# The second mixture's first product as 15 block products over two weight tiles, three depth blocks and three groups of 256 tokens

## The chip, the cores and the metric

The kernel runs on one core of a Trainium2 chip. The metric is the device time of one execution in microseconds (us). The engines' names in the rows are: PE is TensorE (matmuls; PEld are its weight loads), DVE is VectorE, ACT is ScalarE, POOL is GpSimd, SP is SyncE, which here only issues transfers.

## What is computed

Three stages follow each other. A recurrent attention over B=4 sequences of S=768 tokens (8 heads of 48) gives 3072 rows of 384. The first mixture multiplies two products of these rows elementwise and takes them through two more matrices. The second mixture, which the change is about, has E=8 experts of 1024 hidden units and a gate that is normalised over rows and columns in turn, eight times (the Sinkhorn iterations):

```python
a = x @ w1                     # first mixture, x is 3072 x 384, w1 and w2 384 x 1024
b = x @ w2
x = (a * b @ w3) @ w_out       # 3072 x 384
...
logits = x @ w_gate            # second mixture, E = 8
P = np.exp(logits - logits.max())
for _ in range(8):
    P /= P.sum(1, keepdims=True) + 1e-09
    P /= P.sum(0, keepdims=True) + 1e-09
    P *= N / E
for e in range(E):
    h = np.maximum(x @ w1[e], 0.0)         # 3072 x 384 @ 384 x 1024
    out += P[:, e:e + 1] * (h @ w2[e])     # 3072 x 1024 @ 1024 x 384
```

All is float32. Each product of two blocks is made of three matmuls, since each factor is kept as a high part (rounded by ScalarE) and a low part (what is left, by GpSimd or VectorE): high by high, high by low, low by high.

## The kernel before

**The second mixture** is a loop over N=96 phases (expert e, slab sb, half dp). A slab is 512 tokens, 256 of each of two sequences; there are six. A weight tile i holds the columns of w1[e] and the rows of w2[e] for 256 hidden units; an expert has four, and a half has two. In a phase TensorE makes the hidden units of one slab for two weight tiles (called z, in PSUM tiles `zp`, three banks of 128 partitions by 512) and multiplies those of the phase before by w2 (called y, tiles `yp`). The depth 384 is three blocks of 128. Over two of the depth blocks, the two row blocks that a weight tile has and the two token groups, z goes by the seven products of Strassen's scheme in Winograd's form (P1 to P7); the third depth block adds four plain products (R11 to R22). That is 11 block products for each of the two tiles, 66 matmuls of 256 columns in a phase. y has 16 units of three matmuls of 384 columns. `phase` writes the order of TensorE out by hand: after each product `slot()` lets one queued piece of other work (`ex`) and one step of the Sinkhorn iterations (`sk`, from the third phase on) be issued, and `y_units(k)` puts k units of y between the products, so that the evacuation of a PSUM bank passes behind them.

**Evacuation.** ScalarE copies the first product of a phase out (`t`, L802) and takes the relu with rounding (`hh`, L779); VectorE forms the sums of the scheme (`u`, `vv`, `cc`, L786), the low halves (`hl`, L783) and, every second phase, four accumulations of y times the gate (`acc`, L894).

**Preparation of factors.** Both sides of the scheme need sums of blocks. For a weight tile `sp_w1a` makes four sums of 128x128 on GpSimd (L574 to L577), and `sp_w1b`, issued some slots later, the high halves on ScalarE (L591) and the low halves on GpSimd (L592): nine forms. For a slab of x, `sp_x_a` makes four sums of 128x256 on GpSimd (L619 to L622) and `sp_x_b` the high (L632) and low halves (L633), nine forms too. These are made once for each slab, in the first expert's phases (the first slab's at the end of the first mixture), stored to DRAM (`xd`) and loaded again into `xc` for each later expert, into two tiles in turn, 2304 KB a load. w2 is split by ScalarE (L605) and VectorE (L606).

**The end of the first mixture.** The last block of 384 tokens goes through eight slices (s=99 to 106), in each of which TensorE makes `pa` and `pb`, ScalarE copies `asb` (L423) and rounds `gh` (L437), VectorE multiplies `gs` (L436) and GpSimd makes `gl` (L438). Four more slices (s=107 to 110) make 72 matmuls `po` from `gh` and `gl`; the last three of their first third and the other 48 need the last `gl`. Beside this the first weight tiles and the first slab are prepared, in the order in which the slices are written.

Each engine works off its own instructions in the order written; a wait in one holds all that stand behind it on that engine. `reuse_waits="tile"` lets a tile's next use wait only for the last use of that tile.

## Time and profile before

| | us |
|---|---|
| device time, median of 3 runs | 2074.86 (2073.59 to 2075.13) |
| the profiled execution | 2072.34 |
| its span in the trace | 2070.2 |
| second mixture on TensorE: first z to last y | 502.14 to 2066.67 |
| one phase in steady state | 16.22 |

The span is the time from the first to the last instruction of the trace; 2.14 us of the profiled execution lie outside it. All times in the rows count from the span's start.

### The profile page before, as it was taken

To read this page: it belongs to the slowest core of one execution; us is meant where nothing else is said; L and a number is where in the kernel's file an instruction comes from. 1 tells how busy PE (TensorE), PEld (TensorE's weight loads), DVE (VectorE), ACT (ScalarE), POOL (GpSimd) and SP (SyncE) were. 2 spreads that over 40 slices of the span, in tenths; PEclk is the share of its full clock that TensorE was granted. 3 is DMA by queue.
4 is the path that set the end of the run, shared out by engine and by line. 5 is a ranking of instruction groups with operands and counts; after the bars stand their busy time and mean duration, and the time that the engine had idled before them with its cause. 6 is when DMAs were issued, how large, how long until landed. Compare 5 with 4: busy or idle time off the path is not lost.

```text
span 2070.2 us, 37109 instructions
## 1 busy us (share of the span) xinstructions
PE 2004.5 (97%) x16075; PEld 1954.4 (94%) x16075; DVE 1145.3 (55%) x1782; ACT 531.1 (26%) x916; POOL 487.4 (24%) x487
## 2 busy tenths in 40 slices
...
GB/s 251 182 141 94 89 91 100 102 40 92 107 92 92 108 92 47 91 152 47 92 63 137 91 47 128 73 91 92 108 92 47 92 152 47 92 63 122 106 78 31
DMA packets 45827, 199.55 MB, mean 96 GB/s; under 512 B 6176, under 2 KB 16480, under 8 KB 38496
## 3 DMA queue, kind: packets, MB, share of 16 engines
...
## 4 chain that ended last, share of the span: by engine, by line
PE 92%; DVE 5%; POOL 1%; issue 1%; ACT 1%; DMA 1%; SPq 0%; DVEq 0%; ACTq 0%; POOLq 0%
...
## 5 line engine op out<-in xcount | busy, mean ns | idle before, releaser
L84 PE MATMUL zp<-xc,w1h 128*128 128x256 f32 x4224 | 781.9, 280 | 0.9 <-ACT t L802 0.9
L84 PEld LDWEIGHTS zp<-xc,w1h 128*128 128x128 f32 x4224 | 691.3, 188 | 2.0 <-ACT t L802 1.4
L84 PE MATMUL zp<-xc,w1l 128*128 128x256 f32 x2112 | 594.2, 281 | 0.0
L84 PE MATMUL yp<-w2h,hh 128*128 128x384 f32 x1536 | 517.8, 337 | 0.0
L84 PE MATMUL yp<-w2l,hh 128*128 128x384 f32 x1536 | 516.6, 336 | 0.6 <-DVE w2l L606 0.6
L84 PE MATMUL yp<-w2h,hl 128*128 128x384 f32 x1536 | 516.2, 336 | 0.0
L84 PEld LDWEIGHTS zp<-xc,w1l 128*128 128x128 f32 x2112 | 398.1, 189 | 0.0
L779 ACT ACTIVATE hh<-cc 128x512 fp32r<-128x512 f32 x288 | 182.2, 633 | 797.6 <-DVE cc L786 797.6
L592 POOL TENSOR_TENSOR w1l<-w1raw,w1h 128x768 fp32r<-128x768 f32 x32 | 59.2, 1851 | 1087.8 <-ACT w1h L591 1087.8
L84 PEld LDWEIGHTS yp<-w2h,hh 128*128 128x128 f32 x1536 | 289.7, 189 | 0.4 <-issue 0.2
L84 PEld LDWEIGHTS yp<-w2l,hh 128*128 128x128 f32 x1536 | 288.8, 188 | 0.9 <-DVE w2l L606 0.9
L84 PEld LDWEIGHTS yp<-w2h,hl 128*128 128x128 f32 x1536 | 288.3, 188 | 0.0
L786 DVE TENSOR_TENSOR cc<-u,zp 128x512 f32<-128x512 f32 x192 | 131.9, 687 | 269.1 <-PE zp L84 269.1
L786 DVE TENSOR_TENSOR u<-t,zp 128x512 f32<-128x512 f32 x192 | 132.0, 688 | 200.0 <-PE zp L84 164.6
L783 DVE SCALAR_TENSOR_TENSOR hl<-cc,hh 128x512 fp32r<-128x512 f32 x288 | 198.7, 690 | 7.2 <-ACT hh L779 7.1
L894 DVE SCALAR_TENSOR_TENSOR acc<-yp,Pm,acc 128x384 f32<-128x384 f32 x168 | 103.4, 616 | 116.8 <-PE yp L84 116.8
L779 ACT ACTIVATE hh<-zp 128x512 fp32r<-128x512 f32 x96 | 57.5, 599 | 257.1 <-PE zp L84 257.1
L783 DVE SCALAR_TENSOR_TENSOR hl<-zp,hh 128x512 fp32r<-128x512 f32 x96 | 65.9, 686 | 74.5 <-ACT hh L779 74.3
L438 POOL TENSOR_TENSOR gl<-gs,gh 128x384 fp32r<-128x384 f32 x64 | 84.4, 1318 | 96.3 <-ACT gh L437 96.2
L84 PE MATMUL pa<-xhl,w1h 128*128 128x384 f32 x384 | 105.3, 355 | 1.4 <-DVE xhl L405 0.8
L84 PE MATMUL pb<-xhl,w2h 128*128 128x384 f32 x384 | 98.7, 338 | 1.9 <-ACT w2h L198 1.9
L786 DVE TENSOR_TENSOR vv<-u,zp 128x512 f32<-128x512 f32 x96 | 66.0, 688 | 49.8 <-PE zp L84 49.7
...
## 6 DMA issues: line engine op xcount, KB each, us to landing
xc<-xd SPq DMA_DIRECT2D x42, 2304.0 KB, 8.8
xd<-xc SPq DMA_DIRECT2D x6, 2304.0 KB, 6.9
...
```

What stands on the lines that cost most here:

```text
L84: nc.tensor.matmul(o, lhsT, rhs, start=start, stop=stop, **kw)
L438: nc.gpsimd.tensor_tensor(gl[:, f, :], gs, gh[:, f, :].bitcast(F32), op=ALU.subtract)
L592: nc.gpsimd.tensor_tensor(lo[:, d0:d0 + n, :], src, hi[:, d0:d0 + n, :].bitcast(F32), op=ALU.subtract)
L779: nc.scalar.activation(hh, src, AF.Relu)
L783: nc.vector.scalar_tensor_tensor(hl, src, 0.0, hh.bitcast(F32), op0=ALU.max, op1=ALU.subtract)
L786: nc.vector.tensor_tensor(o, a, b_, op=ALU.add)
L894: nc.vector.scalar_tensor_tensor(dst, ya[t], Pm[:, tt, e:e + 1], dst, op0=ALU.mult, op1=ALU.add)
```

## The change

z is made by a scheme of 15 block products over a matrix of 2 by 3 blocks (two row blocks of a weight tile, three depth blocks) and one of 3 by 3 (three depth blocks, three groups of 256 tokens), where plain multiplication needs 18. A slab is now one whole sequence, 768 tokens; there are 16 pairs of weight tiles (k) by four slabs (sb), so N=64 phases. A phase has 15 products of 6 matmuls (128x256) and 24 units of y of 3 matmuls (128x384). `ORDER` is the order of the products, `WA` and `XC` say which blocks make the two factors of each. The products fall into four groups by that order (four, four, four, three); the factor forms of a group lie in one tile (`w1c{k}{g}`, `xc{g}`).

What moves with it:

- `combine` and `split` now stand together: a call of `sp_w1(i, g)` or `sp_x(sb, g)` issues the sums of a group on GpSimd and the high and low halves right behind, first those of plain blocks, then those of sums. The sums go through one temporary tile (`w1s` or `tx`), which the next group reuses. A weight tile takes 12 sums of 128x128 and 1920 columns of low halves, a slab 15 sums of 128x256 and 3840 columns.
- There is one set of `xc` tiles. `release(n, g)` stands at the last product of a group: in the first three phases it queues `sp_x` for the next slab's group, and from then on it issues the load of that group from DRAM, 60 times four loads of 1024, 1024, 1024 and 768 KB.
- `sp_w1(2k+2, g)` is queued for the first four products of a phase with sb=1 (of the fourth phase for k=0), `sp_w1(2k+3, g)` at the releases of a phase with sb=3. The first tile and the first slab are prepared at slices 99 to 103, the second tile at 107 to 110.
- Several products take turns in one bank, each evacuated before the next: 8, 9 and 10 (ScalarE copies), 5, 2 and 13, 11 and 3, 6 and 7, 12 and 1. z has four banks, y three in rotation, and y is accumulated to `acc` in every phase (six times, 384 in all, where there were 192).
- VectorE has 13 sums, six low halves and six accumulations a phase, ScalarE four copies and six relus. A Sinkhorn step is issued behind every second product from the second phase on.

On ScalarE, at the end of the first mixture, before (`w1h` high halves of weights, `asb` and `gh` as above):

```order
L591 ACTIVATE w1h_5580<-w1raw 128x768
L423 ACTIVATE asb<-pa 128x384
L437 ACTIVATE gh<-gs 128x384
L591 ACTIVATE w1h_5580<-w1s 128x384
L423 ACTIVATE asb<-pa 128x384
L437 ACTIVATE gh<-gs 128x384
```

and after, in the slices s=101 to 103 (`tx` and `w1s` are the sums that GpSimd makes, `x2s` the slab's plain blocks):

```order
L424 ACTIVATE asb<-pa 128x384
L438 ACTIVATE gh<-gs 128x384
L618 ACTIVATE w1c_5657<-w1raw 128x256
L618 ACTIVATE w1c_5657<-tx_5522 128x128
L618 ACTIVATE xc_5665<-x2s 128x256
L618 ACTIVATE xc_5665<-tx_5522 128x768
L424 ACTIVATE asb<-pa 128x384
L438 ACTIVATE gh<-gs 128x384
L618 ACTIVATE xc_5703<-tx_5522 128x768
L424 ACTIVATE asb<-pa 128x384
```

Between two slices' `asb` there stand now up to four high halves, of which those from `tx` follow sums that GpSimd makes in the same slice.

On ScalarE, at the start of the second mixture, before:

```order
L779 ACTIVATE hh<-zp 128x512
L632 ACTIVATE xc<-x2s 128x1280
L632 ACTIVATE xc<-tx 128x1024
L779 ACTIVATE hh<-cc 128x512 x3
L802 ACTIVATE t_6179<-zp 128x512
```

and after (`ct` are the copies and sums of z):

```order
L802 ACTIVATE hh<-ct 128x512 x3
L618 ACTIVATE xc_6073<-x2s 128x256
L618 ACTIVATE xc_6073<-tx 128x768
L802 ACTIVATE hh<-ct 128x512 x3
L618 ACTIVATE xc_6121<-tx 128x768
L817 ACTIVATE ct<-zp 128x512 x3
```

The last group of the next slab stands now right ahead of the copies with which the next phase begins.

On ScalarE, in a later phase with weights to prepare, before:

```order
L802 ACTIVATE t_7737<-zp 128x512
L591 ACTIVATE w1h_7739<-w1raw 128x768
L591 ACTIVATE w1h_7739<-w1s 128x384
L779 ACTIVATE hh<-zp 128x512
L591 ACTIVATE w1h_7781<-w1raw 128x768
L591 ACTIVATE w1h_7781<-w1s 128x384
L779 ACTIVATE hh<-cc 128x512 x3
```

and after, in a phase with sb=1:

```order
L817 ACTIVATE ct<-zp 128x512
L618 ACTIVATE w1c_7342<-w1s 128x512
L817 ACTIVATE ct<-zp 128x512
L618 ACTIVATE w1c_7365<-w1raw 128x128
L618 ACTIVATE w1c_7365<-w1s 128x384
L817 ACTIVATE ct<-zp 128x512
L618 ACTIVATE w1c_7391<-w1raw 128x128
L618 ACTIVATE w1c_7391<-w1s 128x384
L618 ACTIVATE w1c_7415<-w1raw 128x256
L618 ACTIVATE w1c_7415<-w1s 128x128
L817 ACTIVATE ct<-zp 128x512
```

The copies of z stand now between the high halves of sums that GpSimd makes in the same phase. The core of the diff:

```diff
-        return x2[(b // 2) * NR + t0 // T][:, SLOT[q, b % 2], :], t0 % T
+        return x2[b][:, SLOT[q, t0 // T], :], t0 % T
...
+    ORDER = (8, 9, 10, 5, 2, 13, 11, 6, 3, 15, 12, 7, 1, 14, 4)
+    WA = {8: "-10+11", 9: "+00-10+11", 10: "-00+01+10-11", 5: "-01+02",
+          2: "+01-02+12", 13: "+12", 11: "+00-02", 6: "-01+02+11-12", 3: "+02-12", 15: "-10+12", 12: "-00+12",
+          7: "+11", 1: "-00+10", 14: "+00", 4: "+01"}
+    XC = {8: "+01", 9: "-01+12", 10: "+12", 5: "+21", 2: "+10+21", 13: "+00+20-21", 11: "+22", 6: "+10",
+          3: "+10+20+22", 15: "+00", 12: "-00+22", 7: "+01-10+11", 1: "+00+02+12", 14: "+01+02+22", 4: "+11+12+21"}
+    WB = ((0, 0), (0, 1), (1, 1), (1, 2), (0, 2), (1, 0))
...
+    def combine(groups, g, blocks, raw, tmp_):
+        many, one, s0, steps, pos = groups[g]
+
+        def at_(x):
+            return tmp_[:, x[1], :] if x[0] == "c" else raw[:, blocks.index(x[1]), :]
+
+        for r, a, b, sg in steps:
+            nc.gpsimd.tensor_tensor(tmp_[:, many.index(r), :], at_(a), at_(b), op=ALU.add if sg == 1 else ALU.subtract)
+
+    def split(groups, g, raw, tmp_, hi, lo):
+        many, one, s0, steps, pos = groups[g]
+        nm, no = len(many), len(one)
+        for d0, d1, sv in ((nm, nm + no, raw[:, s0:s0 + no, :]), (0, nm, tmp_[:, 0:nm, :])):
+            if d1 > d0:
+                nc.scalar.activation(hi[:, d0:d1, :], sv, AF.Copy)
+                nc.gpsimd.tensor_tensor(lo[:, d0:d1, :], sv, hi[:, d0:d1, :].bitcast(F32), op=ALU.subtract)
...
+    def sp_w1(i, g, tmp_=None):
...
-        t = w1raw[i]
-        c = pools[0].tile([P, 3, P], F32, tag="w1s", bufs=2, name="w1s")
-        a21, a11, a12, a22 = (t[:, j, :] for j in range(4))
-        g = nc.gpsimd
-        g.tensor_tensor(c[:, 1, :], a11, a21, op=ALU.subtract)
-        g.tensor_tensor(a21, a21, a22, op=ALU.add)
-        g.tensor_tensor(c[:, 0, :], a21, a11, op=ALU.subtract)
-        g.tensor_tensor(c[:, 2, :], a12, c[:, 0, :], op=ALU.subtract)
-        sw[i] = c
...
-    def sp_w1b(i, part):
...
-        nc.scalar.activation(hi[:, d0:d0 + n, :], src, AF.Copy)
-        nc.gpsimd.tensor_tensor(lo[:, d0:d0 + n, :], src, hi[:, d0:d0 + n, :].bitcast(F32), op=ALU.subtract)
...
+        n_ = len(WP_[g][4])
+        k = i % 3
+        if tmp_ is None:
+            tmp_ = pools["m"].tile([P, 4, P], F32, tag="w1s", bufs=1, name="w1s")
+        t = pools["w" if k == 0 else "m"].tile([P, 2, n_, P], F32R, tag=f"w1c{k}{g}", name=f"w1c{k}{g}")
+        w1c[i, g] = t
+        combine(WP_, g, WB, w1raw[i], tmp_)
+        split(WP_, g, w1raw[i], tmp_, t[:, 0], t[:, 1])
...
-        hi = pools[1].tile([P, 2, DM], F32R, tag=f"w2h{p}", name=f"w2h{p}")
-        lo = pools[1].tile([P, 2, DM], F32R, tag=f"w2l{p}", name=f"w2l{p}")
+        k = i % 4
+        pool = pools["m" if k == 0 else "m2"]
+        hi = pool.tile([P, 2, DM], F32R, tag=f"w2h{k}", name=f"w2h{k}")
+        lo = pool.tile([P, 2, DM], F32R, tag=f"w2l{k}", name=f"w2l{k}")
         nc.scalar.activation(hi, t, AF.Copy)
         nc.vector.tensor_tensor(lo, t, hi.bitcast(F32), op=ALU.subtract)
...
-    def sp_x_a(si, t):
-        x = x2[si]
-        b12, b11, b21, b22 = (x[:, j, :] for j in range(4))
-        g = nc.gpsimd
-        g.tensor_tensor(t[:, 0, :], b12, b11, op=ALU.subtract)
-        g.tensor_tensor(t[:, 2, :], b22, b12, op=ALU.subtract)
-        g.tensor_tensor(t[:, 1, :], b22, t[:, 0, :], op=ALU.subtract)
-        g.tensor_tensor(t[:, 3, :], b21, t[:, 1, :], op=ALU.subtract)
-        tx_[si] = t
...
-        d0, src = ((0, x[:, 1:, :]), (5, tx_[si]))[part]
-        n = src.shape[1]
-        nc.scalar.activation(h[:, 0, d0:d0 + n, :], src, AF.Copy)
-        nc.gpsimd.tensor_tensor(h[:, 1, d0:d0 + n, :], src, h[:, 0, d0:d0 + n, :].bitcast(F32), op=ALU.subtract)
-        if part == 1:
-            xd[si] = dram.tile([P, 2, 9, T], F32, name=f"xd{si}")
-            nc.sync.dma_start(xd[si], h.bitcast(F32))
...
+    def sp_x(sb, g, tmp_=None):
+        t = x_tile(sb, g)
+        if tmp_ is None:
+            tmp_ = pools["m"].tile([P, 4, T], F32, tag="tx", name="tx")
+        combine(XP_, g, XB, x2[sb], tmp_)
+        split(XP_, g, x2[sb], tmp_, t[:, 0], t[:, 1])
+        xd[sb, g] = dram.tile(list(t.shape), F32, name=f"xd{sb}{g}")
+        nc.sync.dma_start(xd[sb, g], t.bitcast(F32))
...
+    def ld_x(n, g):
+        if n >= NB2 * NS:
             return
-        xc[si] = x_tile(si)
-        nc.sync.dma_start(xc[si].bitcast(F32), xd[si % NS])
+        t = x_tile(n, g)
+        nc.sync.dma_start(t.bitcast(F32), xd[n % NS, g])
...
+        if 4 * NU + UB <= s < 4 * NU + UB + NGR:
+            if s == 4 * NU + UB:
+                tx0 = moe.tile([P, 6, T], F32, tag="xraw", name="tx0")
+            g = s - (4 * NU + UB)
+            sp_w1(0, g, tx0[:, 4:6, :].rearrange("p a (b c) -> p (a b) c", c=P))
+        if 4 * NU + UB + 1 <= s < 4 * NU + UB + 1 + NGR:
+            sp_x(0, s - (4 * NU + UB + 1), tx0[:, 0:4, :])
+        if s == NSL - X2S:
...
+        if s >= NSL - X2S:
+            sp_w1(1, s - (NSL - X2S))
+        if s == NSL - 1:
             ld_w2(0)
             ld_w2(1)
-        if s == 4 * NU + 2:
-            sp_w1a(0)
-            sp_w1b(0, 0)
-        if s == 4 * NU + 3:
-            sp_w1b(0, 1)
-        if s == 4 * NU + 4:
-            sp_w1a(1)
-            sp_w1b(1, 0)
-        if s == 4 * NU + 5:
-            sp_w1b(1, 1)
-        if s == 4 * NU + 7:
-            sp_w1a(2)
-        if s == 4 * NU + 8:
-            sp_w1a(3)
-        if s == NSL - 4:
-            sp_x_a(0, moe.tile([P, 4, T], F32, tag="xraw", name="tx0"))
-        if s == NSL - 3:
-            sp_x_b(0, 0)
-        if s == NSL - 2:
-            sp_x_b(0, 1)
...
-        return ps2.tile([P, 2, T], F32, tag="z", bufs=3, name="zp")
...
+        return ps2.tile([P, 2, T], F32, tag="z", bufs=4, name="zp")
...
+    YN = dict(zip(ORDER, (2, 2, 1, 2, 2, 1, 1, 1, 2, 1, 2, 2, 2, 1, 99)))
...
+        def after(r):
+            if ORDER.index(r) % 4 == 3 or r == ORDER[-1]:
+                release(n, GOF[r])
+            if ex:
+                ex.popleft()()
+            if sk and at["sk"] and ORDER.index(r) % 2:
+                sk.popleft()()
+            y_units(YN[r])
...
+        def s8():
+            prod("b", 8, True, True)
+            ct["8"] = cp(bk["b"])
...
+        def s9():
+            prod("b", 9, False, True)
+            ct["12"] = cp(bk["b"])
+
+        def s10():
+            prod("b", 10, False, True)
+            ct["02"] = cp(bk["b"])
+
+        def s5():
+            prod("a", 5, True, True)
...
+            sub(ct["01"], bk["a"], ct["02"])
+
...
+            prod("a", 2, False, True)
+            sub(ct["8"], bk["a"], ct["8"])
+
+        def s13():
+            prod("a", 13, False, True)
+            ct["00"] = cp(bk["a"])
+
+        def s11():
+            prod("g", 11, True, True)
...
+            prod("e", 7, False, True)
+            add(ct["8"], ct["8"], bk["e"])
+            h_hi(n, 1, 1, ct["8"])
+            h_lo(n, 0, 0)
...
+            h_hi(n, 0, 1, ct["01"])
+            h_lo(n, 0, 2)
+
...
-            b1 = z_new()
-            z_prod(b1, n, "P1", True, True)
-            t1 = tmp_t("t1")
-            nc.scalar.activation(t1, b1, AF.Copy)
-            slot()
-        y_units(2)
-        if z:
-            b2 = z_new()
-            z_prod(b2, n, "P6", True, True)
-            u2 = tmp_t("u2")
-            add(u2, t1, b2)
...
+        def unit(b_, h_, i, j):
+            first = i == 1 and j == 0
+            last = i == 0 and j == 1
+            if first:
+                yt[b_, h_] = ps2.tile([P, DM], F32, tag="y", bufs=3, name="yp")
...
-                if e == 0:
...
+                if k == 0:
...
+                    nc.vector.scalar_tensor_tensor(dst, yp, Pm[:, tt, e:e + 1], dst, op0=ALU.mult, op1=ALU.add)
...
+        for b_ in (0, 2, 1):
+            for h_ in range(2):
+                for i in (1, 0):
+                    for j in range(2):
+                        yq.append(lambda b_=b_, h_=h_, i=i, j=j: unit(b_, h_, i, j))
...
+    def release(n, g):
+        if n >= N:
+            return
+        k, sb = divmod(n, NS)
+        if n + 1 < NS:
+            ex.append(lambda: sp_x(n + 1, g))
+        else:
+            ld_x(n + 1, g)
+        if sb == NS - 1:
+            ex.append(lambda: sp_w1(2 * k + 3, g))
+
+    CT, HB = 8, 8
...
-            w0 = e * NPR
-            if sb == 0 and dp == 0:
-                ex.extend([lambda i=i, k=k: sp_w1b(i, k) for i in (w0 + 2, w0 + 3) for k in range(2)])
-                ex.extend([lambda i=i: sp_w2(i) for i in (w0, w0 + 1)])
-            if sb == 0 and dp == 1:
-                ex.extend([lambda i=i: sp_w2(i) for i in (w0 + 2, w0 + 3)])
-            if sb == NS - 1 and dp == 0:
-                for i in (w0 + 4, w0 + 5):
-                    sp_w1a(i)
-            if sb == NS - 1 and dp == 1:
-                ex.extend([lambda i=i, k=k: sp_w1b(i, k) for i in (w0 + 4, w0 + 5) for k in range(2)])
-                ex.extend([lambda i=i: sp_w1a(i) for i in (w0 + 6, w0 + 7)])
-            if e == 0 and sb + 1 < NS:
-                if dp == (1 if sb == 0 else 0):
-                    ex.append(lambda si=si: sp_x_a(si + 1, m2.tile([P, 4, T], F32, tag="tx", name="tx")))
-                    ex.extend([lambda si=si, k=k: sp_x_b(si + 1, k) for k in range(2)])
...
+            if n == 0:
+                ex.extend([lambda i=i: sp_w2(i) for i in (0, 1)])
+            if 2 * NS <= n < 3 * NS:
+                ex.extend([lambda sb=sb, t=t: rescale(sb, t) for t in range(S // P)])
+            if sb == (NS - 1 if k == 0 else 1):
+                ex.extend([lambda i=2 * k + 2, g=g: sp_w1(i, g) for g in range(NGR)])
+            if sb == 2:
+                ex.extend([lambda i=i: sp_w2(i) for i in (2 * k + 2, 2 * k + 3)])
+        at["sk"] = n >= 1
...
```

## Rows read from the trace of the kernel before

**Rows 1.** Page, busy time, share of the span, instructions; then the chain's shares.

```profile
PE 2004.5 (97%) x16075; PEld 1954.4 (94%) x16075; DVE 1145.3 (55%) x1782; ACT 531.1 (26%) x916; POOL 487.4 (24%) x487
...
PE 92%; DVE 5%; POOL 1%; issue 1%; ACT 1%; DMA 1%; SPq 0%; DVEq 0%; ACTq 0%; POOLq 0%
```

**Rows 2.** Chain of waits: start, length, engine, tile, line, instructions.

```profile
1490.20 2.08 PE yp L84 x12
1506.42 2.11 PE yp L84 x12
...
2056.25 10.42 PE yp L84 x60
```

**Rows 3.** PE timeline: start, length, engine, line, operation, out<-in, shape, count.

```profile
502.14 0.40 PE L84 MATMUL zp<-xc,w1h 128*128 128x256 f32 x2
...
548.15 0.40 PE L84 MATMUL zp<-xc,w1h 128*128 128x256 f32 x2
...
548.86 0.34 PE L84 MATMUL yp<-w2h,hh 128*128 128x384 f32 x1
```

**Rows 4.** POOL timeline at the first mixture's end; brackets: idle before, and releaser.

```profile
468.17 1.02 POOL L438 TENSOR_TENSOR gl<-gs,gh 128x384 fp32r<-128x384 f32 x1 [1.21 <-ACT gh L437]
...
472.81 0.46 POOL L575 TENSOR_TENSOR w1raw<-w1raw 128x128 f32<-128x128 f32 x1
473.34 0.46 POOL L576 TENSOR_TENSOR w1s<-w1raw 128x128 f32<-128x128 f32 x1
...
491.15 1.01 POOL L438 TENSOR_TENSOR gl<-gs,gh 128x384 fp32r<-128x384 f32 x1 [2.10 <-ACT gh L437]
492.12 0.74 POOL L619 TENSOR_TENSOR tx<-x2s 128x256 f32<-128x256 f32 x1
...
495.81 2.96 POOL L633 TENSOR_TENSOR xc<-x2s,xc 128x1280 fp32r<-128x1280 f32 x1 [0.74 <-ACT xc L632]
499.76 2.40 POOL L633 TENSOR_TENSOR xc<-tx,xc 128x1024 fp32r<-128x1024 f32 x1 [0.99 <-ACT xc L632]
```

**Rows 5.** ACT timeline there: a high half that waits, and what stands behind.

```profile
473.30 0.84 ACT L591 ACTIVATE w1h<-w1raw 128x768 fp32r<-128x768 f32 x1 [2.08 <-POOL w1raw L575]
474.05 0.47 ACT L423 ACTIVATE asb<-pa 128x384 f32<-128x384 f32 x1
```

**Rows 6.** Busy time by stretch: PE, PEld, DVE, ACT, POOL, granted clock, DMA share, GB/s.

```profile
116.00:118.00 2.00, 0.00 (x0) 0.00 (x0) 0.01 (x1) 1.96 (x3) 1.04 (x1) 0.99 0.44 104
118.00:120.00 2.00, 0.60 (x22) 0.60 (x25) 1.89 (x4) 0.57 (x2) 2.00 (x3) 0.50 0.69 289
```

**Rows 7.** POOL and DVE timelines at the second mixture's start.

```profile
512.17 1.45 POOL L621 TENSOR_TENSOR tx<-x2s,tx 128x256 f32<-128x256 f32 x1
...
511.97 1.05 DVE L606 TENSOR_TENSOR w2l<-w2raw,w2h 128x768 fp32r<-128x768 f32 x1 [1.44 <-ACT w2h L605]
```

**Rows 8.** ACT and PE timelines: the one bank that TensorE waited for.

```profile
515.39 0.58 ACT L802 ACTIVATE t<-zp 128x512 f32<-128x512 f32 x1
...
516.02 0.51 PE L84 MATMUL zp<-xc,w1h 128*128 128x256 f32 x2 [0.86 <-ACT t L802]
```

**Rows 9.** Waits of PE: line, waited for, us in total, times, longest.

```profile
PE pcs L84 <- DVE cs L935: 3.3, 6, 0.8
```

**Rows 10.** DVE timeline: three operations that followed without a gap.

```profile
1521.41 0.68 DVE L783 SCALAR_TENSOR_TENSOR hl<-cc,hh 128x512 fp32r<-128x512 f32 x1
1522.02 0.61 DVE L894 SCALAR_TENSOR_TENSOR acc<-yp,Pm,acc 128x384 f32<-128x384 f32 x1
1522.56 0.69 DVE L786 TENSOR_TENSOR cc<-vv,zp 128x512 f32<-128x512 f32 x1
```

**Rows 11.** PE and DVE timelines: a bank's last matmul, and its evacuation.

```profile
1501.93 0.28 PE L84 MATMUL zp<-xc,w1l 128*128 128x256 f32 x1
...
1502.24 0.69 DVE L786 TENSOR_TENSOR cc<-u,zp 128x512 f32<-128x512 f32 x1 [1.80 <-PE zp L84]
```

**Rows 12.** Page, DMA issues: tiles, operation, count, KB each, us to landing.

```profile
xc<-xd SPq DMA_DIRECT2D x42, 2304.0 KB, 8.8
```

319 lines of the change are left out of this document (153 added, 166 removed).

## The prediction

> **What bounds the kernel now.** I read the page's busy times and shares of the chain first [rows 1]: TensorE is busy 97% of the span and holds 92% of the chain that ended last, so only matmuls that are saved, or time in which TensorE has to wait, can move the end. Then the chain itself [rows 2]: in the second mixture it runs through TensorE alone, the last units of y of each phase standing 16.22 us apart (1490.20 to 1506.42). The timeline of TensorE gives the prices [rows 3]: six z matmuls take 548.86 − 548.15 = 0.71 us (0.1185 each), and the 60 y matmuls that end the chain take 10.42 us [rows 2], 0.52 for a unit of three. A phase of 11 × 0.71 + 16 × 0.52 = 16.17 us is within 0.3% of what is seen, so the steady state has no waits. From the first z at 502.14 [rows 3] to 2056.25 + 10.42 = 2066.67 [rows 2] are 1564.5 us; 96 × 16.17 are 1552. The 12 us between are the start of the mixture and the Sinkhorn steps.
>
> **What is removed.** z falls from 96 × 66 = 6336 to 64 × 90 = 5760 matmuls of the same shape, y stays at 4608. That is 576 × 0.1185 = **68.2 us** less on the engine that bounds. A new phase has 15 × 0.71 + 24 × 0.52 = 23.2 us of TensorE, and there are 64. All that follows is what may eat this up.
>
> **Preparation at the first mixture's end.** Before, GpSimd had 4 + 4 sums and nine forms of x in this stretch; now its queue, from the first `gl` of the last block on (468.17, done at 469.2 [rows 4]), holds ahead of the last `gl`: seven `gl` of 0.97 (491.15 to 492.12) = 6.8; 12 weight sums of 0.54 (472.81 to 473.34) = 6.5; 1920 columns of weights' low halves at 0.97 for 384, with a little for their smaller pieces, = 5.0; 15 sums of x of 0.74 = 11.1; 3840 columns of x's low halves at 2.96 for 1280 and 2.40 for 1024 = 9.0. That makes 38.4. To this come waits for ScalarE's high halves: seen are 0.74 and 0.99 [rows 4]. Sums and halves are issued together, so a high half on ScalarE waits for GpSimd in turn, and `asb` and `gh` of the next slice stand behind it; the trace has one such case, a high half held 2.08 us by GpSimd with `asb` right behind [rows 5]. Of the waits some three us fall into GpSimd's chain by my walk through the two queues. The last `gl` then ends near 469.2 + 41.4 = 510.6. Before, z started 502.14 − 492.12 = 10.0 us after it (two and 48 `po` matmuls, which need it, and what lies around them); the same puts z at 520.6, **18.5 us** later. TensorE has 18 matmuls to do in a slice in which GpSimd has up to 8 us, so it stands idle between. After such a gap the granted clock fell: with no matmul from 116 to 118 it was 0.50, the lower of its two levels (1.2 GHz), in the next 2 us [rows 6]. At half speed over half the `po` I add 2.5. **+21 us**; between +15 (no waits, clock full) and +27 (seven high halves of x and four of weights held about 0.9 each, as the two seen).
>
> **Start of the second mixture.** Phase 0 has no y: 10.7 us of TensorE. Meanwhile GpSimd prepares the second slab: 15 × 0.74 + 9.0 = 20.1 us, behind what is left of the second weight tile. One row prices a disturbance: a sum beside VectorE's `w2l` took 1.45 us for 0.74 [rows 4, 7]; VectorE will have some six such operations beside GpSimd in a phase, at 0.4 held each +2.4 (my choice, between 0 and 6 × 0.71). The Trainium skill ("GPSIMD Engine Reference", section 1) says that GpSimd's SBUF interfaces are shared with VectorE and contended by its operations with two SBUF inputs; the row agrees. If each of these held GpSimd for its whole length, as that rule can be read, three phases would cost some 4 us more, 30 for the 26 below.
> ScalarE's queue decides what this costs. The copy of product 8 of the next phase stands behind the high half of the old phase's last x group, which needs that group's six sums. So phase 1 gets past its second product only near 29 us after the first z, where 10.7 + 1.75 = 12.4 us would do: 17. In phases 1 and 2 the same 20.1 + 2.4 and the waits between the engines stand against 23.2 us of TensorE, and the hand-over at the phase's end is late by some 5.5 and 3.5 us. Phase 3 prepares two weight tiles in slots next to each other: 4.7. The Sinkhorn steps share VectorE and the column bank; before, TensorE waited six times, 3.3 us in all, for one of them [rows 9]; with half as many slots a phase and more of VectorE's time taken I put 7 on three phases and a rest. Together 38, less the 12 that before had: **+26 us**, from +14 (GpSimd unhindered, phases 1 to 3 hidden) to +36 (each wait as long as the 2.08 seen).
>
> **Weights in later phases.** For 14 pairs, four calls of `sp_w1` follow each other in a phase with sb=1. GpSimd makes the first sums ahead, but the second group's sums need the one temporary tile, so they wait for the first's low half: 512 columns, 1.3 us, then four sums, 2.2 us. ScalarE's high half of the second group waits for that, and the copy of product 10 stands behind it: it starts some 4.6 us after the first copy instead of 3.5. That is late for product 5's sum and so for product 2, which follows in its bank: 0.9 a phase, 14 × 0.9 = **+12.6 us**; nothing, if the sums are done in time, +20 if the third and fourth groups hold a copy too.
>
> **In-bank chains.** A bank shared by products in turn is a new wait in every phase. After a bank's last matmul started, VectorE started on it 0.31 us later (1501.93 to 1502.24 [rows 11]) and takes 0.69; ScalarE takes 0.58 to 0.60, and TensorE resumed 0.05 after it (515.39 + 0.58 to 516.02 [rows 8]). That is 1.05 or 0.96 us. Between two products of one bank stand at least two units of y and the last z matmul, 2 × 0.52 + 0.12 = 1.16 us. Slack is 0.11 or 0.20, so I put 0. VectorE has 19 operations of 0.61 and six of 0.54 (1521.41 to 1522.02 to 1522.56 [rows 10]), 14.8 of 23.2 us; in the second half of a phase it works without pause, and just in time.
>
> **Transfers.** 3840 KB a phase in four loads; a load of 2304 KB took 8.8 us in the median [rows 12], so 14.7 of 23.2 us go to them. A group has some 17 us from its release to its next use and takes 3.9 for 1024 KB. Hidden: 0.
>
> **Small.** Four phases with six rescales of VectorE, at some 0.5 a phase, and 15 phases with sb=3 whose releases carry a weight group, 0.1 each: **+3.5**.
>
> **Sum.** −68.2 + 21 + 26 + 12.6 + 3.5 = −5.1 us. The profiled execution (2072.34, its span 2070.2 plus 2.14) would be 2067.2. The median of the runs shown is 2.5 above it, 2074.86: **2069.8 us**.
>
> **The rivals.**
> - *Preparation half hidden.* TensorE has queued work to cover waits where my walk through the queues adds them: GpSimd's first sums run ahead of their slot. If only half of 63 us reaches TensorE: 2074.86 − 68.2 + 31.6 = 2038. For it: in before the same kinds of wait (2.08 us at a high half [rows 5]) hardly moved TensorE. Against: that was a slab of nine forms, with its sums issued slots ahead.
> - *Preparation dearer by a third*, by GpSimd held as in the 1.45 row each time and ScalarE's queue passing it on: 2069.8 + 21 = 2091.
> - *Banks come free too late* (slower than before). If the evacuation is later than its slack at the four tightest places of a phase by 0.1 us, this costs 4 × 64 × 0.1 = 26, 2095; by 0.2, 51, 2121. From 0.036 us on it is slower than before by more than 0.2%. For it: slack of 0.11 beside a VectorE that works without pause, and the one bank wait of the trace, 0.86 us for `t` [rows 8]. Against: that one stands at the start, with ScalarE busy on weights. The Trainium skill ("Perfetto Trace Analysis", Optimizing Tensor Performance, Matmuls) lets independent groups of matmuls rotate through different PSUM banks, so that one's evacuation runs beside the next's matmuls; the chains 8, 9, 10 and 5, 2, 13 in one bank each go against that, and by it this rival is where the time would go. No row of before shows such a chain in steady state.
> - *Loads too slow.* If a phase's 3840 KB took more than the 23.2 us, each us over costs 60. At the rate seen there is room for a factor of 1.5.
> - That the change does not do what it says is excluded by the counts: the new order has 5760 z matmuls.
>
> **How the numbers follow.** Forecast as reckoned, 2058 to 2081: 0.45. Preparation half hidden, near 2038: 0.22. A third dearer, near 2091: 0.16. Banks late, 2095 and up: 0.12. Loads: 0.05. The range goes from 2034 to 2096; outside are the worse part of the banks' case, the loads and a little below. Within 0.2%, about what a measurement of this kernel can tell from no change, is 2070.7 to 2079.0: of the forecast 0.19 falls there, 0.02 above, 0.24 below. Faster 0.24 + 0.22 = 0.46, same 0.19, slower 0.02 + 0.16 + 0.12 + 0.05 = 0.35. The forecast's own range of both signs is 2058 to 2081.
>
> **What would show it.** Phases of 23.2 us in steady state, without waits of z for `ct`, show that the banks hold; phases with sb=1 near 24.1, waiting for a copy. The first z near 521 after the span's start, the chain passing through GpSimd and ScalarE ahead of it; phase 1 past its second product near 29 us later. A first z near 505 and phases 1 to 3 of 23.2 would make the prediction wrong towards 2038; steady phases of 23.6 or more, with z waiting for `ct` each time, towards 2095.

## The result and the profile after

The changed kernel takes 2085.57 us in the median of six runs (2083.02 to 2087.6), the kernel before 2073.92 in the runs beside it. The ratio is 1.0055 with an interval of 1.0044 to 1.0066: **slower by 0.55%**, 11.7 us, where some 5 us less was forecast. The profiled execution has a span of 2085.9 us, 15.7 more than before; the sums below are made against this, and since it is the slowest of the six, and that of before (2072.34) faster than all six beside it, they come out some 4 us higher than the medians.

The page after, with busy times, shares of the chain, the group of the z matmuls (count, busy time, mean ns, then idle time before it) and the loads of x, beside [rows 1, 12]:

```profile
PE 1968.2 (94%) x15499; PEld 1894.9 (91%) x15499; DVE 1402.5 (67%) x2242; ACT 667.4 (32%) x1252; POOL 727.7 (35%) x955
...
PE 78%; DVE 8%; POOL 7%; ACT 4%; issue 2%; DMA 1%; SPq 0%; DVEq 0%; POOLq 0%; ACTq 0%
...
L83 PE MATMUL zp<-xc,w1c 128*128 128x256 f32 x5760 | 851.8, 284 | 39.9 <-ACT ct L817 28.7
...
xc<-xd SPq DMA_DIRECT2D x180, 1024.0 KB, 4.8
```

The group of z matmuls that waited in before:

```profile
L84 PE MATMUL zp<-xc,w1h 128*128 128x256 f32 x4224 | 781.9, 280 | 0.9 <-ACT t L802 0.9
```

TensorE's share of the chain that ended last fell from 92 to 78%, and what it lost went to VectorE, GpSimd and ScalarE. The z matmuls had 0.9 us of idle time ahead of them in before and have 39.9 now, most of it for a copy of z. Waits of TensorE after (us in total, times, longest):

```profile
PE zp L83 <- ACT ct L817: 28.7, 17, 10.4
...
PE pa L83 <- ACT asb L424: 10.5, 3, 5.4
PE zp L83 <- DVE ct L813: 9.8, 15, 1.1
...
PE pb L83 <- ACT asb L424: 3.7, 1, 3.7
```

The waits for `asb` stand at the first mixture's end, nearly all of those for ScalarE's copies (L817) at the start of the second, and 13 of the 15 for VectorE's sum (L813) in phases with sb=1 (the other two in phase 0). No wait is for a load of x.

The phases are read from the timeline of TensorE, from the first of each 90 z matmuls to the next (the work is 10.7 us in phase 0 and 23.2 in the others; all in us; the columns from w2 on are the experiments below):

| | after | w2 early | no x | x ahead | w1 ahead | y moved | all | Sinkhorn later |
|---|---|---|---|---|---|---|---|---|
| first z | 525.5 | 525.8 | 525.2 | 525.5 | 524.8 | 525.1 | 508.8 | 509.5 |
| phase 0 | 23.8 | 16.4 | 23.8 | 23.8 | 22.3 | 23.7 | 19.5 | 17.4 |
| 1 | 38.4 | 37.9 | 28.5 | 29.6 | 38.3 | 38.3 | 29.5 | 29.5 |
| 2 | 30.0 | 29.1 | 24.1 | 28.6 | 30.0 | 30.0 | 28.5 | 25.2 |
| 3 | 34.9 | 34.9 | 26.9 | 32.2 | 31.0 | 34.0 | 26.4 | 27.3 |
| 4 | 25.6 | 25.6 | 25.3 | 25.3 | 25.4 | 25.0 | 25.9 | 24.6 |
| 5 | 25.2 | 25.2 | 25.2 | 25.2 | 23.9 | 24.7 | 23.8 | 24.3 |
| 24 (sb=0) | 23.67 | 23.64 | 23.66 | 23.67 | 23.66 | 23.14 | 23.14 | 23.14 |
| 25 (sb=1) | 24.06 | 24.05 | 24.05 | 24.12 | 23.27 | 23.56 | 23.23 | 23.16 |
| 26 | 23.29 | 23.29 | 23.29 | 23.29 | 23.27 | 23.16 | 23.16 | 23.23 |

The 15.7 us come together so: −68.2 of z matmuls; +23.3 for the first z (525.48 against 502.14); +39.7 for phases 0 to 6 (51.9 over their work, against the 12.2 of before); +20.6 for phases 7 to 62 (12 with sb=1 lose 0.78 each, 14 with sb=0 0.41, phase 10 0.96, and each phase 0.08). The rest is rounding.

**The first mixture's end**, ScalarE's timeline after:

```profile
497.44 0.84 ACT L618 ACTIVATE xc<-tx 128x768 fp32r<-128x768 f32 x1 [4.14 <-POOL tx L611]
498.19 0.47 ACT L424 ACTIVATE asb<-pa 128x384 f32<-128x384 f32 x1
...
505.66 0.84 ACT L618 ACTIVATE xc<-tx 128x768 fp32r<-128x768 f32 x1 [5.79 <-POOL tx L611]
506.41 0.47 ACT L424 ACTIVATE asb<-pa 128x384 f32<-128x384 f32 x1
```

A high half waits 5.79 us for GpSimd's sums, and the copy `asb`, whose input is long there, goes only behind it: the 2.08 of [rows 5], grown. TensorE's matmuls of the next slice wait in turn:

```profile
498.71 1.01 PE L83 MATMUL pa<-xhl,w1h 128*128 128x384 f32 x2 [5.41 <-ACT asb L424]
506.94 1.01 PE L83 MATMUL pa<-xhl,w1h 128*128 128x384 f32 x2 [2.92 <-ACT asb L424]
...
512.86 0.47 PE L83 MATMUL po<-gh,w34h 128*128 128x384 f32 x1
```

From 506.94 to the first z TensorE works without a pause: the 18 matmuls of the last slice, at the lower clock, take 5.9 us, the 72 `po` behind them 12.6.

**The second mixture's start**, TensorE:

```profile
525.48 0.88 PE L83 MATMUL zp<-xc,w1c 128*128 128x256 f32 x6
...
532.85 2.93 PE L83 MATMUL zp<-xc,w1c 128*128 128x256 f32 x12 [4.49 <-ACT ct L817]
...
561.59 1.65 PE L83 MATMUL zp<-xc,w1c 128*128 128x256 f32 x6 [10.41 <-ACT ct L817]
```

Two waits stand out. ScalarE at both:

```profile
531.47 0.84 ACT L660 ACTIVATE w2h<-w2raw 128x768 fp32r<-128x768 f32 x1 [4.14 <-DMA w2raw<-in_e_w_dram]
532.22 0.58 ACT L817 ACTIVATE ct<-zp 128x512 f32<-128x512 f32 x1
...
560.21 0.84 ACT L618 ACTIVATE xc<-tx 128x768 fp32r<-128x768 f32 x1 [6.04 <-POOL tx L611]
560.96 0.58 ACT L817 ACTIVATE ct<-zp 128x512 f32<-128x512 f32 x1
```

The second is the one foreseen: the copy of product 8 behind the last x group. The first was not. The load of w2 that ScalarE waits for stands on SyncE's queue, here its issues (start, and the time from the first to the last issue):

```profile
527.36 0.33 SPq L627 DMA_DIRECT2D w1raw<-in_e_w_dram  x1
527.75 7.15 SPq L634 DMA_DIRECT2D w2raw<-in_e_w_dram  x4
```

Ahead of it stands the load of the fourth weight tile, whose buffer GpSimd reads until 527.3. The change issues the w2 loads in the last slice, behind that one; before, they were issued 15 slices earlier.

### The profile page after: what moved, and what is told of

Its sections match the earlier page's. It is cut to its first block, busy times and chain, and to the rows that moved or that the text cites. A ratio compares the mean times of both kernels' runs of the same rounds, so it can differ in the third digit from the quotient of the medians.

```text
span 2085.9 us, 37865 instructions
## 1 busy us (share of the span) xinstructions
PE 1968.2 (94%) x15499; PEld 1894.9 (91%) x15499; DVE 1402.5 (67%) x2242; ACT 667.4 (32%) x1252; POOL 727.7 (35%) x955
## 4 chain that ended last, share of the span: by engine, by line
PE 78%; DVE 8%; POOL 7%; ACT 4%; issue 2%; DMA 1%; SPq 0%; DVEq 0%; POOLq 0%; ACTq 0%
PE yp L83 32%; PE zp L83 29%; PE po L83 4%; PE pa L83 4%; PE pb L83 4%; POOL tx L611 2%; DVE ct L810 2%; POOL w1s L611 1%; ACT hh L802 1%; ACT ct L817 1%; PE yt L83 1%; POOL w1c L619 1%; DVE hl L807 1%; POOL xc L619 1%; ACT w1c L618 1%
## 5 line engine op out<-in xcount | busy, mean ns | idle before, releaser
L83 PE MATMUL zp<-xc,w1c 128*128 128x256 f32 x5760 | 851.8, 284 | 39.9 <-ACT ct L817 28.7
L83 PEld LDWEIGHTS zp<-xc,w1c 128*128 128x128 f32 x5760 | 797.8, 191 | 64.2 <-ACT ct L817 37.8
L810 DVE TENSOR_TENSOR ct<-ct,zp 128x512 f32<-128x512 f32 x576 | 381.9, 684 | 67.5 <-PE zp L83 64.2
L802 ACT ACTIVATE hh<-ct 128x512 fp32r<-128x512 f32 x384 | 237.6, 633 | 584.4 <-DVE ct L810 294.1
L619 POOL TENSOR_TENSOR w1c<-w1s,w1c 128x512 fp32r<-128x512 f32 (+1 forms) x124 | 124.4, 1004 | 855.4 <-ACT w1c L618 820.6
L807 DVE SCALAR_TENSOR_TENSOR hl<-ct,hh 128x512 fp32r<-128x512 f32 x384 | 280.1, 743 | 2.5 <-ACT hh L802 2.4
L817 ACT ACTIVATE ct<-zp 128x512 f32<-128x512 f32 x256 | 152.5, 596 | 323.4 <-PE zp L83 319.2
L950 DVE SCALAR_TENSOR_TENSOR acc<-yp,Pm,acc 128x384 f32<-128x384 f32 x336 | 205.4, 611 | 63.2 <-PE yp L83 63.0
L813 DVE TENSOR_TENSOR ct<-ct,zp 128x512 f32<-128x512 f32 x128 | 88.1, 688 | 172.8 <-PE zp L83 172.7
L813 DVE TENSOR_TENSOR ct<-zp,ct 128x512 f32<-128x512 f32 x128 | 88.6, 692 | 150.9 <-PE zp L83 119.0
L611 POOL TENSOR_TENSOR w1s<-w1raw 128x128 f32<-128x128 f32 x248 | 115.0, 485 | 9.6
```

Source lines behind the costliest of these rows:

```text
L83: nc.tensor.matmul(o, lhsT, rhs, start=start, stop=stop, **kw)
L611: nc.gpsimd.tensor_tensor(tmp_[:, many.index(r), :], at_(a), at_(b), op=ALU.add if sg == 1 else ALU.subtract)
L619: nc.gpsimd.tensor_tensor(lo[:, d0:d1, :], sv, hi[:, d0:d1, :].bitcast(F32), op=ALU.subtract)
L802: nc.scalar.activation(hh, src, AF.Relu)
L807: nc.vector.scalar_tensor_tensor(hl, src, 0.0, hh.bitcast(F32), op0=ALU.max, op1=ALU.subtract)
L810: nc.vector.tensor_tensor(o, a, b_, op=ALU.add)
```

## The experiments

**w2 loaded early.**

```diff
             pools["m"] = ctx.enter_context(tc.tile_pool(name="m1", bufs=1, side="right", reuse_waits="tile"))
+            ld_w2(0)
+            ld_w2(1)
         if s >= NSL - X2S:
             sp_w1(1, s - (NSL - X2S))
-        if s == NSL - 1:
-            ld_w2(0)
-            ld_w2(1)
```

> Edit: the first two loads of w2 are issued three slices earlier, ahead of the load of a weight tile that has to wait for GpSimd. Theory of the held load: in the trace of the changed kernel ScalarE waited 4.14 us for w2raw with the copy of product 9 behind it, and TensorE 4.49 us before product 10; the transfer stood on SyncE's queue behind a load whose buffer GpSimd freed at 527.3. Then this wait goes and all that follows moves up: 4 to 5 us less, 2081. Rival, that GpSimd's own chain paces the start anyway: the wait turns up again at the second phase's copies, and the time stays within 1 us of 2085.6.

Measured: 2078.69, 6.9 us less (ratio to before 1.0020, 1.0010 to 1.0029). The loads are issued at 511.59 now, the wait of 4.49 us falls to 0.69 and phase 0 from 23.8 to 16.4. The theory of the held load holds; the gain is larger than the wait, since the granted clock had been at the lower of its two levels behind it. The twelve matmuls that stand behind the wait took 2.93 us in the changed kernel (the line of 532.85) and take 1.69 here:

```profile
529.44 1.69 PE L83 MATMUL zp<-xc,w1c 128*128 128x256 f32 x12 [0.69 <-ACT ct L816]
```

Windows in phase 0, first of the changed kernel, then all of phase 0 of this one (length; busy time of PE, PEld, DVE, ACT and POOL; granted clock; DMA share, GB/s):

```profile
530.00:544.00 14.00, 9.52 (x41) 8.93 (x42) 4.61 (x6) 5.12 (x9) 4.66 (x5) 0.51 0.50 179
```

```profile
525.80:542.10 16.30, 12.26 (x91) 11.04 (x91) 9.81 (x15) 9.25 (x18) 12.56 (x15) 1.00 0.52 186
```

With 0.51 for 14 us the one, with 1.00 throughout the other: of the 7.4 us by which phase 0 is shorter some 3.7 are waits, and 3.7 matmuls that go faster. The clock in phase 0 does not hang on this wait alone: in the run with all edits, which has no wait of this length there, it was 0.74 (below). TensorE is past the next wait, the one behind the last x group, 28.7 us after the first z (554.47), where it was 36.1 (561.59).

**No x forms for three slabs.**

```diff
-        nc.sync.dma_start(t.bitcast(F32), xd[n % NS, g])
+        nc.sync.dma_start(t.bitcast(F32), xd[0, g])
...
-        xt = xc[n, g]
+        xt = xc[n if n >= NS else 0, g]
...
-            ex.append(lambda: sp_x(n + 1, g))
+            pass
```

> Edit: the forms of the second, third and fourth slab are not made at all; phases 0 to 3 read the first slab's forms, and later loads take these too (the computation of three of four sequences is left out in this sense). It isolates what preparing x costs in the first phases. In the changed kernel the phases 0 to 6 were 51.9 us over their TensorE work (13.1, 15.2, 6.8, 11.7, 2.4, 2.0, 0.7). Theory that ScalarE's queue behind GpSimd's sums sets the start: phases 1 and 2 fall to 23.2 to 23.5, the clock stays at full from phase 1 on, some 24 us less in all, near 2061. Rival, that the start is paced by hand-overs without cover and by the low clock that the tail of the first mixture leaves: phases 1 and 2 keep half of their 22 us, near 2073.

Measured: 2063.35 in one run, 22 us less. Phases 1 to 3 fall by 9.9, 5.9 and 8.0 us: preparing x costs some 24 of the 51.9 us at the start. Phase 1 keeps 5.3 us over its work; those were expected to go, and the clock to be full from there on (it was 0.94 over phase 1). TensorE's timeline shows what they are:

```profile
552.67 0.97 PE L83 MATMUL zp<-xc,w1c 128*128 128x256 f32 x6 [1.75 <-ACT ct L817]
553.57 1.45 PE L83 MATMUL pl<-x2s,gate 128*32 128x128 f32 x18
...
555.44 0.52 PE L83 MATMUL yp<-w2l,hh 128*128 128x384 f32 x1
```

A wait for the copy of product 8 takes 1.75 us. The 18 matmuls of the gate's logits (`pl`) and four small ones of the first Sinkhorn steps, which the 23.2 us do not contain, take 1.8. The rest is matmuls at the lower clock behind the wait, as the y matmul of 0.52 us, which takes 0.34 later on. A second thing shows in VectorE's low halves of z in phase 1, first of the changed kernel, then of this one (count, shortest/median/longest in ns):

```profile
L807 DVE SCALAR_TENSOR_TENSOR hl<-ct,hh x7: 680/1205/1886, 549.6 to 585.3; 128x512 fp32r<-128x512 f32 x7
```

```profile
L807 DVE SCALAR_TENSOR_TENSOR hl<-ct,hh x7: 680/681/685, 549.0 to 574.5; 128x512 fp32r<-128x512 f32 x7
```

With GpSimd idle every `hl` takes 0.68 us; beside its sums and halves the median is 1.2.

**Sums of x two groups ahead.** Two temporary tiles for one; the same instructions in another order. `sp_xa` makes only the sums of a group, at the start of a phase those of the first two; `sp_x` now makes only the halves:

```diff
-            ex.append(lambda: sp_x(n + 1, g))
+            def step():
+                sp_x(n + 1, g)
+                sp_xa(n + 1, g + 2)
+            ex.append(step)
...
-    CT, HB = 8, 8
+    CT, HB = 7, 8
...
+            if n + 1 < NS:
+                sp_xa(n + 1, 0)
+                sp_xa(n + 1, 1)
```

> Edit: the sums of a slab's groups are issued on GpSimd up to two groups ahead of their high and low halves, through two temporary tiles instead of one (one of the eight tiles for copies of z is given up for it). GpSimd does the same work. Theory of ScalarE's queue: the high halves no longer wait for sums, so the copies behind them don't: the wait of 10.4 us in phase 1 falls under 3, phases 1 to 3 fall by 12 to 18 us together, near 2070. Rival, GpSimd's throughput of 20 us a slab paces phases 0 to 2: the waits only move to the products whose low halves are late, at most 5 us less, 2081 or more.

Measured: 2072.90, 12.7 us less (0.9996 of before, 0.9987 to 1.0006). The wait of phase 1 on TensorE:

```profile
554.15 1.65 PE L83 MATMUL zp<-xc,w1c 128*128 128x256 f32 x6 [2.93 <-ACT ct L825]
```

From 10.41 to 2.93 us, as the theory of ScalarE's queue had it. GpSimd does the same work, so its throughput was not what phase 1 waited for in the main. The gain in phases 1 to 3 is 8.8, 1.4 and 2.7, together 12.9, at the lower end of what was expected.

**Sums of weights two groups ahead.** Here too one of the eight tiles for copies of z is given up:

```diff
-            ex.append(lambda: sp_w1(2 * k + 3, g))
-
-    CT, HB = 8, 8
+            if g == 0:
+                ex.append(lambda: (sp_w1a(2 * k + 3, 0), sp_w1a(2 * k + 3, 1)))
+            ex.append(lambda: (sp_w1(2 * k + 3, g), sp_w1a(2 * k + 3, g + 2)))
+
+    CT, HB = 7, 8
...
-                ex.extend([lambda i=2 * k + 2, g=g: sp_w1(i, g) for g in range(NGR)])
+                ex.append(lambda i=2 * k + 2: (sp_w1a(i, 0), sp_w1a(i, 1)))
+                ex.extend([lambda i=2 * k + 2, g=g: (sp_w1(i, g), sp_w1a(i, g + 2)) for g in range(NGR)])
```

> Edit: the same for the weight tiles from the third on: their sums go to GpSimd two groups ahead of the halves, through two temporary tiles. Theory that the high halves on ScalarE hold the copies of product 10 (sb=1) and of product 8 (sb=0): the phases with sb=1 fall from 24.06 to 23.3 and those with sb=0 from 23.69 to 23.3, together 15 us, and phase 3 by 3 more: 2068. Rival, that the loss in these phases is VectorE's or the loads': they stay at 24.06 and 23.69, 2083 to 2086.

Measured: 2069.41, 16.2 us less (0.9977, 0.9968 to 0.9986). In the changed kernel a phase with sb=1 went so on ScalarE and TensorE:

```profile
1156.96 0.53 ACT L618 ACTIVATE w1c<-w1s 128x384 fp32r<-128x384 f32 x1 [1.68 <-POOL w1s L611]
1157.40 0.58 ACT L817 ACTIVATE ct<-zp 128x512 f32<-128x512 f32 x1
```

```profile
1158.76 0.98 PE L83 MATMUL zp<-xc,w1c 128*128 128x256 f32 x6 [0.36 <-DVE ct L813]
```

The high half waits 1.68 us for sums, the copy of product 10 goes behind it, VectorE's sum of product 5 needs that copy and product 2 needs the bank. With the sums ahead these phases take 23.27 instead of 24.06, and phase 3 takes 31.0 instead of 34.9. Those with sb=0 stay at 23.66, so that half of the theory falls. Their start in the changed kernel shows why:

```profile
1128.73 0.40 ACT L618 ACTIVATE w1c<-w1raw 128x256 fp32r<-128x256 f32 x1
1129.04 0.30 ACT L618 ACTIVATE w1c<-w1s 128x128 fp32r<-128x128 f32 x1
1129.23 0.58 ACT L817 ACTIVATE ct<-zp 128x512 f32<-128x512 f32 x1
```

Nothing waits here: two high halves, 0.5 us of ScalarE's own work, stand ahead of the copy of product 8.

**The tail's sums on VectorE.** `combine` and `split` take an engine, so that the low halves of the first slab move too:

```diff
-            sp_w1(0, g, tx0[:, 4:6, :].rearrange("p a (b c) -> p (a b) c", c=P))
+            sp_w1(0, g, tx0[:, 4:6, :].rearrange("p a (b c) -> p (a b) c", c=P), nc.vector)
...
-            sp_x(0, s - (4 * NU + UB + 1), tx0[:, 0:4, :])
+            sp_x(0, s - (4 * NU + UB + 1), tx0[:, 0:4, :], nc.vector)
...
-            sp_w1(1, s - (NSL - X2S))
+            sp_w1(1, s - (NSL - X2S), None, nc.vector)
```

> Edit: in the last slices of the first mixture the sums of the first two weight tiles and of the first slab, and the slab's low halves, are made by VectorE, which was busy 2 us in 20 there; GpSimd keeps the weights' low halves and gl. Theory that the chain of sums on GpSimd, and ScalarE's high halves that wait for it with asb behind, delays the first z: it starts at 503 to 507 instead of 525.5, no matmul of pa waits 5 us for asb, the clock stays at full there, and 18 to 24 us go from the time: 2062 to 2068. Rival, that ScalarE's own work or the loads hold the first z: it stays later than 515 and at most 10 us go.

Measured: 2068.26, 17.3 us less (0.9975, 0.9963 to 0.9986). The first z is at 508.76, a little later than the 503 to 507 expected, and two waits of `pa` are left:

```profile
487.49 0.62 PE L83 MATMUL pa<-xhl,w1h 128*128 128x384 f32 x2 [2.77 <-ACT asb L424]
493.03 0.62 PE L83 MATMUL pa<-xhl,w1h 128*128 128x384 f32 x2 [2.11 <-ACT asb L424]
```

16.7 of the 23.3 us went with the sums and the slab's low halves, so the chain through GpSimd's sums and ScalarE's queue was the tail's price.

**A unit of y moved; the last weight group later.**

```diff
-    YN = dict(zip(ORDER, (2, 2, 1, 2, 2, 1, 1, 1, 2, 1, 2, 2, 2, 1, 99)))
+    YN = dict(zip(ORDER, (2, 2, 1, 3, 2, 1, 1, 1, 1, 1, 2, 2, 2, 1, 99)))
...
         if sb == NS - 1:
+            if g == NGR - 1:
+                ex.extend([lambda: None] * 3)
             ex.append(lambda: sp_w1(2 * k + 3, g))
```

> Two edits that show in different places. One unit of y is moved from behind product 3 to behind product 5, where in each phase the next product of the same bank started 0.08 to 0.09 us late; and at the end of a phase with sb=3 the halves of the last weight group are issued three products later, behind product 10 of the next phase, so that ScalarE does not have them ahead of the copy of product 8. Theory: the step behind product 2 loses 0.09 in each of 64 phases, steady phases go from 23.27 to 23.18 (5.5 us), and those with sb=0 from 23.69 to 23.2 (14 of them, 6 us more): 2074. Rival, that VectorE's pace sets the phase: the same 0.09 turns up at another product, and 2080 to 2086 remains.

Measured: 2067.28, 18.3 us less (0.9964, 0.9950 to 0.9978), more than expected. The steady phases (sb=2 and 3) fall from 23.27 to 23.19 in the mean, those with sb=0 from 23.67 to 23.14, as expected; those with sb=1 fall too, from 24.06 to 23.56. That the unit behind product 5 covers a part of its late sum there would give such a gain; no run separates it. The 0.09 is the one in-bank hand-over without slack. VectorE and TensorE in the changed kernel:

```profile
1275.57 0.69 DVE L813 TENSOR_TENSOR ct<-zp,ct 128x512 f32<-128x512 f32 x1
```

```profile
1276.34 0.95 PE L83 MATMUL zp<-xc,w1c 128*128 128x256 f32 x6
```

Product 5's sum ends at 1275.57 + 0.69 = 1276.26, and product 2 starts at 1276.34 with a first matmul that is drawn out (0.95 for six instead of 0.87). At products 9, 10 and 13 nothing is late.

**Waits filled with matmuls without use.**

```diff
-            if start:
+            if start and not (r == 5 and "a" in bk):
                 bk[nm] = z_new()
...
             ct["8"] = cp(bk["b"])
+            for _ in range({1: 60, 2: 24, 3: 30}.get(n, 0)):
+                if "a" not in bk:
+                    bk["a"] = z_new()
+                mm(bk["a"][:, 0, :], w1c[(n // NS) * 2, 0][:, 0, 0, :], xc[n, 0][:, 0, 0, :], True, True, skip=True)
```

> Edit: matmuls without use are put behind product 8 in phases 1, 2 and 3 (60, 24 and 30 of 128x256, 7.1, 2.8 and 3.5 us at full clock), into a bank that is free, where TensorE waited 10.4, 3.5 and 4.6 us for a copy; nothing else changes. It asks what the lower clock after a wait costs. In the changed kernel the clock was at its lower level for 13.7 us after the wait of phase 1 and for 6.8 and 10.2 us in phases 2 and 3. Theory that this is part of the start's loss: with the wait filled the lower level goes there, phase 1 falls by 4 to 7 us and phases 2 and 3 by 1 to 4 each: 2072 to 2080. Rival, that GpSimd and VectorE set the pace there and TensorE's lost half would be waited for anyway: phases 1 to 3 stay within 1 us of 38.4, 30.0 and 34.9.

Measured: 2084.61, 1.0 us less, which is within the spread of either kernel's runs. Phases 1 to 3 take 37.5, 27.8 and 34.9, the added matmuls among it. Windows, of the changed kernel over phases 1 and 2, then of this one, columns as above:

```profile
549.20:587.60 38.40, 27.99 (x186) 26.72 (x186) 21.37 (x35) 11.54 (x20) 27.87 (x29) 0.82 0.28 116
587.60:617.60 30.00, 26.49 (x169) 25.99 (x167) 23.41 (x46) 12.70 (x21) 21.92 (x22) 0.89 0.39 150
```

```profile
547.00:585.00 38.00, 34.40 (x250) 33.30 (x249) 21.48 (x35) 11.32 (x20) 28.61 (x30) 0.96 0.30 123
585.00:614.00 29.00, 28.30 (x203) 27.60 (x202) 24.82 (x49) 13.04 (x22) 23.27 (x24) 1.00 0.43 168
```

The granted clock is near full now, and the phases are 0.8, 2.2 and 0 us shorter. Phase 2 goes by the theory. Phase 3 goes by the rival: its matmuls take some 3 us less, but waits of the same length come up behind them. Phase 1 decides little, since its wait was filled only in part and the lower clock came back behind what was left:

```profile
559.96 0.98 PE L83 MATMUL zp<-xc,w1c 128*128 128x256 f32 x6 [3.60 <-ACT ct L817]
...
562.39 0.52 PE L83 MATMUL yp<-w2l,hh 128*128 128x384 f32 x1
```

The mean clock of a phase also overstates what the lower level costs. In phase 1 of the changed kernel more than half of the time at the lower level lay in the wait itself, where TensorE had nothing to do:

```profile
554.00:561.60 7.60, 0.01 (x1) 0.01 (x1) 3.31 (x3) 1.50 (x3) 6.33 (x8) 0.51 0.34 138
561.60:567.90 6.30, 6.30 (x37) 5.60 (x38) 0.85 (x2) 0.60 (x1) 2.08 (x2) 0.51 0.31 125
```

Only the second stretch, 6.3 us at half speed, could be won, some 3 us. What full clock in all of phase 1 would bring is not shown.

**All edits together** (w2 early, x and weights ahead, tail on VectorE, y moved, last group later):

> Edits of the runs before together: w2 loaded early, the sums of x and of weights two groups ahead, the tail's sums on VectorE, one y unit moved, the last weight group later. By the single runs (6.9, 12.7 and 16.2 us measured; 20 and 11 expected) the sum is 67 us; the early load and the tail overlap by some 4, the start's parts by some 5: near 2027. If the losses only move from one wait to the next, more than half comes back and the time stays over 2050.

Measured: 2026.60, 0.9767 of before (0.9752 to 0.9782), 59.0 us less than the changed kernel and as expected. The single gains as measured sum to 71.4 (6.9, 12.7, 16.2, 17.3 and 18.3); so most of each stays, and the losses did not only move to the next wait. They overlap in part: the phases with sb=1 are shortened by the weights ahead and by the moved unit, each by itself. Left are 6.7 us at the first z and, over their work, 8.8, 6.3, 5.3 and 3.2 in phases 0 to 3:

```profile
528.35:557.80 29.45, 26.73 (x186) 25.48 (x185) 21.44 (x34) 11.38 (x20) 27.48 (x28) 0.94 0.35 140
557.80:586.30 28.50, 25.51 (x168) 25.14 (x168) 25.68 (x46) 12.22 (x20) 22.91 (x22) 0.94 0.44 166
```

In phase 2 VectorE is busy 25.68 of 28.50 us.

**Sinkhorn steps later**, on top of this:

```diff
-            if sk and at["sk"] and ORDER.index(r) % 2:
+            if sk and at["sk"] and (ORDER.index(r) % 2 or r == 8):
...
-        at["sk"] = n >= 1
+        at["sk"] = n >= 3
...
```

> Edit on the kernel with all edits together (2026.6): the Sinkhorn steps begin in phase 3 instead of phase 1, eight in a phase instead of seven. Theory: what is left in phases 1 and 2 (6.3 and 5.3 us over their TensorE work) is VectorE's, which was busy 21.4 of 29.4 and 25.7 of 28.5 us there with low halves of z (hl) that take up to 2.3 us beside GpSimd's work for 0.68 alone; with some 14 steps of 0.2 to 0.5 us each moved to phases in which GpSimd is idle, phases 1 and 2 fall by 2 to 3 us each and phases 4 to 7 gain 0.5 at most: 2021 to 2024. Rival, that ScalarE's queue and GpSimd's 20 us set these phases: they stay within 0.5 us, and the later phases get longer: 2027 to 2030.

Measured: 2021.84, **0.9746 of before (0.9729 to 0.9762)**, the fastest of all. Phase 2 falls by 3.3 us and phase 4 by 1.2; phase 1 stays at 29.5, and phases 3 and 5 to 7 give back 0.9, 0.5, 0.4 and 1.3. Phase 0, whose instructions are the same in both, falls by 2.1: the granted clock over it was 0.90 here and 0.74 in the run before, which is no effect that the edit was meant to have. Phases 1 to 7 together are 1.4 us shorter, so less than half of the 4.8 us between the medians is shown to be the edit's. The Sinkhorn steps, mostly VectorE's work, did lengthen phase 2. Phase 1 is held elsewhere, by the queue that held it before:

```profile
531.11 0.84 ACT L618 ACTIVATE xc<-tx 128x768 fp32r<-128x768 f32 x1 [0.80 <-POOL tx L611]
531.86 0.58 ACT L835 ACTIVATE ct<-zp 128x512 f32<-128x512 f32 x1
```

```profile
532.49 1.65 PE L83 MATMUL zp<-xc,w1c 128*128 128x256 f32 x6 [3.66 <-ACT ct L835]
```

The copy of product 8 still stands behind the high half of the last x group. Its wait is 3.66 of the 6.3 us that phase 1 takes over its work, and the rest is matmuls at the lower clock behind it, as the six that take 1.65 us.

**Sums of x on VectorE**, on top of this:

```diff
-            combine(XP_, g, XB, x2[sb], txs[sb, g])
+            combine(XP_, g, XB, x2[sb], txs[sb, g], nc.vector)
```

> Edit on the run before: the sums of x for the slabs of phases 1 to 3 are made by VectorE (15 of 128x256, some 0.37 us each, 5.5 us a phase), which leaves GpSimd 9 us of low halves in a phase for 20. Theory that the two engines hold each other where both read SBUF: hl goes back from 1.0 to 1.3 us in the mean to under 0.9 in phases 1 and 2, which pays for the 5.5 us, and phases 0 to 3 fall by 2 to 6 us together against the run before. Rival, that VectorE's own work sets the pace there: its 5.5 us come on top, phases 1 and 2 are 3 us longer each.

Measured: 2043.07, 21 us more than the run before; phases 0 to 2 take 28.2, 33.5 and 30.6. The mean `hl` of phase 1 goes to 0.76 (that of phase 2 stays at 1.05), but that is not what counts. VectorE's timeline and TensorE's:

```profile
550.01 0.76 DVE L611 TENSOR_TENSOR tx<-x2s 128x256 f32<-128x256 f32 x2 [2.78 <-POOL xc L619]
```

```profile
553.14 1.65 PE L83 MATMUL zp<-xc,w1c 128*128 128x256 f32 x6 [3.38 <-DVE ct L831]
```

The sums need the temporary tile that GpSimd's low half still reads, and the evacuations of z stand behind them on VectorE: the wait that had been ScalarE's is now VectorE's. Both theories miss this.

## Why the prediction was wrong

The sign was wrong. The time, 2085.57, lies in the whole range (2034 to 2096), but above the forecast's own, 2058 to 2081. The profiled executions are 15.7 us apart where the sum gave −5.1. By its steps:

- **What is removed**: right. Pitch and counts are as reckoned; a phase without disturbance takes 23.27 in the changed kernel and 23.16 once the one in-bank hand-over is covered, where 23.2 was forecast.
- **The first mixture's end**: +23.3 for +21, first z at 525.5 for 523.1. The mechanism was right in kind (ScalarE's queue between GpSimd's sums and `asb`), but not its last link. I let the last `gl` hold the `po`; the last slice's `pa` waited for `asb` and with it all 72 `po`. The 2.5 us for the clock came out, but at another place: the 18 matmuls of the last slice took 5.9 us (506.94 to 512.86), where 18 matmuls at 0.52 for three are 3.1, and the `po` ran at full clock.
- **The start of the second mixture**: +39.7 for +26. **This is the step that failed.** These 13.7 us alone turn −5.1 into +8.6; the other misses together come to +7, which would have ended near +2. The mechanism that I put first was there and is the largest part: the copy behind the last x group, 10.41 us on TensorE, 12.7 gone with the order of the sums. Its size was right as well: with w2 loaded early TensorE is past it 28.7 us after the first z, where I had 29. What was missing is the w2 loads, moved on SyncE's queue behind a load that waits: they were not priced at all, and cost 7.4 us in phase 0. The other 6 lie behind that wait, in the rest of phases 1 to 6: with w2 early they lose 26.7 us there, where 5.5, 3.5, 4.7 and 7, together 20.7, were forecast. Two things that I had not counted were at work there, and no run splits the 6 us between them. The lower clock, which I charged to the tail alone, lengthened the matmuls of phases 1 to 3; filling the waits took 3.0 us off these phases. GpSimd was taken as the one that is held beside VectorE (2.4 us a phase), but VectorE is held as well, its `hl` at 1.2 for 0.68.
- **Weights in later phases**: 0.78 a phase for 0.9, by the chain as told (sums, high half, copy of 10, sum of 5, product 2); 24.06 for the 24.1 that were to show it.
- **In-bank chains**: 0 forecast, 0.085 a phase seen, at one of the four tight places. The rival of late banks, at 0.1 us at each of four places, was some five times too dear. The Trainium skill ("Perfetto Trace Analysis", Optimizing Tensor Performance, Matmuls) has independent groups rotate through different PSUM banks; this scheme goes against that, and with two units of y between the products of a bank it lost some 0.085 us a phase, at one hand-over.
- **Transfers**: right. A group of 1024 KB lands in 4.8 us in the median, for the 3.9 reckoned, and no z matmul waits for one.
- **Small**: 3.5 forecast; phases with sb=0 alone lose 14 × 0.41 = 5.7. I had weighed only waits, and here it is ScalarE's own 0.5 us ahead of a copy.
- A slip in the working, without weight: six operations that hold GpSimd for 0.71 us instead of 0.4 add 1.9 a phase, so 5.6 us in three phases and not 4.

Of the rivals, *preparation dearer by a third* came nearest: it put 2091 with a chance of 0.16. Its nearness is in part luck: the largest single miss was the load of w2, which it does not name, and what GpSimd held beside VectorE adds no run shows by itself.
